# Two early weights converted and split beside the bit steps of attention, with smaller head pools

## The chip, the cores and the metric

The kernel runs on one core of a Trainium2 chip. The metric is device microseconds (us) from the first to the last work of one launch, the median of several runs. Five engines take part, each with its own queue that runs in order: PE (TensorE, matmuls; PEld is its weight load), DVE (VectorE), ACT (ScalarE), POOL (GpSimd) and SP (SyncE, which only issues DMAs here).

## The reference

A hash-masked attention over 2 x 8 heads, 768 positions and 64 channels feeds a gated layer (d_ff 1536) and then a layer with h * cos(h) (d_ff 2048). Weights of the two layers come as float64.

```python
q_bits = (np.einsum('bhsd,dk->bhsk', q, proj) > 0)      # 6 bits a position: its bucket
mask = q_bucket[:, :, :, None] == k_bucket[:, :, None, :]
scores = np.where(mask, scale * np.matmul(q, k.transpose(0, 1, 3, 2)), -1000000000.0)
attn = softmax(scores)                                  # max taken off, sum + 1e-9
x = np.matmul(attn, v)                                  # 2 x 8 x 768 x 64 -> 1536 x 512
gate = 1.0 / (1.0 + np.exp(-(x @ w_gate)))
x = (gate * (x @ w_val)) @ w_out                        # first layer
h = x @ w_in
out = (h * np.cos(h)) @ w_out2                          # second layer
```

## The kernel before

The kernel has two parts, `attention()` and `moe()`, and in both each engine's order of work is the order of the code (a manual schedule); only at the border of the two are matmuls of `moe()` set between the last ones of `attention()`.

**Attention** walks through 96 steps `g`, six for each of 16 heads; one step handles 128 query rows against 768 keys. In a step PE makes the scores of step g + 2 (`scores`, L456 and L459), DVE takes the row minimum of step g + 1 (`rowmax`, tile `mn`, L467), ACT the exponential (`expo`, tile `p`, L474), and POOL normalises three steps later (`norm`, L507, in place on `p`). Seven steps later (`LAG`) PE transposes the normalised tiles (`ptrans`, tile `t`, L523), ACT rounds the transpose to its high part `ph` (L528), DVE subtracts it to get the low part `pl` (L533), and PE multiplies both with the values (`pv`, tile `o`, L543 and L544). Three `p` tiles make one unit of six transposes, and the first transpose of a unit needs all three normalised. When a unit is done ACT copies `o` out (`fin_act`, tile `e`, L553); there is one `o` buffer, so the next unit's first matmul waits for that copy. When two heads are done, POOL adds the halves (`fin_sum`, tile `ef`, L580), ACT rounds them into the high half of `xy` (`fin_hi`, L596) and POOL subtracts for the low half (`fin_lo`, L600).

**Preparing a head** hd (loads `nqk`, transposes `pt`, the bits) is spread over earlier steps by the tables `LOAD_AT`, `TRANS_AT`, `BITS_AT`. At step 6 hd - 8 PE makes the six matmuls of the bits (tile `pb`, L341); one step later DVE turns them into codes (tile `bf`, L326) and SP sends them into the head's tiles with four small DMAs (L363). Six more DMAs (`place`, L323) move the transposed q and k into these tiles. DMAs share eight completion counters in turn, and each waits for the DMA that had its counter before.

**The order within a step** is the list `ORDER` (L21): `Tb LOa ... EXP Ta MIN LATE W HIb ...`. `MIN` is the row minimum, `HIb` a rounding to `ph`, `LATE` the codes, and `W` is `early_weights` (L731).

**Early weights.** A weight tile is loaded as float64 words (`load_raw`), converted (`convert_parts`: ACT makes `wp`, L151; DVE makes `wl`, L155, and joins them into `w`, L160) and split (`wsplit`: ACT rounds to the high part `gh` or `vh`, L123; a subtraction makes `gl` or `vl`, L124). The first two weights are `g0` and `v0`. Before, they are loaded at steps 72 and 74, converted at steps 84 to 92 and split by `moe()`, whose pool `wsp` opens only there:

```python
            WL, WC = (72, 74, 76), 84
            WSTEP = 4
```

**moe()** is a list of items, twelve or more matmuls each (L805, L867, L922), with all conversions and splits in between.

Of the kernel before, what the change touches and what calls it, by code (L numbers as in the profile page):

```python
# [9 lines left out]
F32 = mybir.dt.float32  # L10
F32R = mybir.dt.float32r
# [3 lines left out]
ALU = mybir.AluOpType  # L15
# [3 lines left out]
P = 128  # L19

ORDER = (  # L21
    "Tb LOa COEF NRM PVb EXP Ta MIN LATE W HIb PVa PREP S FIN HIa PVaF LOb".split()
)
LAST = ["COEF", "NRM"] + [name for name in ORDER if name not in ("COEF", "NRM")]
FILL = "COEF NRM MIN EXP LATE W PREP S".split()
# [15 lines left out]
def lsh_attention_glu_moe_cos_moe(  # L41
# [80 lines left out]
    def split(dst_h, dst_l, src, sub):  # L122
        nc.scalar.copy(dst_h, src)  # L123
        sub.tensor_tensor(out=dst_l, in0=src, in1=dst_h.bitcast(F32), op=ALU.subtract)  # L124
# [20 lines left out]
    def convert_parts(key):  # L145
        nm, f, _ = key
        rw = raws.pop(key)
        words = rw.bitcast(I32).rearrange("p (n two) -> p n two", two=2)
        lw, hw = words[:, :, 0], words[:, :, 1]
        pt = wraw.tile([P, 512], F32, tag="wp", name=f"wp_{nm}{f}", bufs=2)  # L150
        nc.scalar.activation(  # L151
            pt, hw.bitcast(F32), AF.Prelu, scale=float(2.0**-112), alpha=float(2.0**32)
        )
        lt = wraw.tile([P, 512], I32, tag="wl", name=f"wl_{nm}{f}", bufs=2)
        nc.vector.tensor_scalar(  # L155
            out=lt, in0=lw, scalar1=29, scalar2=7, op0=ALU.logical_shift_right, op1=ALU.bitwise_and
        )
        yield
        w = wraw.tile([P, 512], F32, tag="we", name=f"w_{nm}{f}", bufs=NWE)
        nc.vector.scalar_tensor_tensor(  # L160
            out=w.bitcast(I32),
            in0=pt.bitcast(I32),
            scalar=3,
            in1=lt,
            op0=ALU.logical_shift_left,
            op1=ALU.bitwise_or,
        )
        wt[key] = w
# [51 lines left out]
    def load_to(n, eng=nc.sync):  # L220
        nonlocal loaded
        while loaded < min(n, len(order)):
            load_raw(order[loaded], eng)
            loaded += 1


    def attention():
        nonlocal done
        parts = None
        with ExitStack() as st:  # L230
            nat = st.enter_context(tc.tile_pool(name="nat", bufs=3))
            prep = st.enter_context(tc.tile_pool(name="prep", bufs=3))
            vsp = st.enter_context(tc.tile_pool(name="vsp", bufs=3))
            pp = st.enter_context(tc.tile_pool(name="pp", bufs=10))
            tiny = st.enter_context(tc.tile_pool(name="tiny", bufs=3))
# [357 lines left out]

            def fin_hi(u):
                for h, _, x in pieces(u):
                    nc.scalar.copy(h, x)  # L596

            def fin_lo(u):
                for h, lw, x in pieces(u):
# [1 line left out]

            LAG = 7

            WL, WC = (72, 74, 76), 84
            WSTEP = 4
            NW = 2 * NG

            todo = {}
# [21 lines left out]
                at(s1 + VALUES_AT[hd % 2], lambda hd=hd: values(hd))  # L630

            late = []

            def run_late():
                now = late[:]
# [33 lines left out]
            with tc.manual_schedule(  # L669
# [50 lines left out]
                for g in range(NG + LAG + 2):  # L720
# [8 lines left out]
                            at(g + LOW_AT + (3 if g < NG <= g + LOW_AT else 0), lambda u=fin: fin_lo(u))  # L729

                    def early_weights():  # L731
                        nonlocal done, parts
                        if g in WL:
                            load_to(1 + WL.index(g), nc.scalar)
                        if done < NEARLY and g >= WC and (g - WC) % WSTEP == 0:
                            parts = convert_parts(order[done])
                        if parts is not None and next(parts, parts) is parts:
                            parts = None
                            done += 1
                        elif parts is None and 0 < done <= NEARLY:  # L740
                            load_to(done + 3, nc.scalar)

                    def norms():
                        for n in range(g - 3, NG if g == NG else g - 2):
# [23 lines left out]
                        "PREP": (True, lambda: run_todo(g)),  # L768
                        "HIa": (0 <= wa + 2 < NW, lambda: phi(wa + 2)),
                    }  # L770
                    for name in ORDER if LAG - 1 <= g != NG else LAST if g == NG else FILL:
                        on, fn = ops[name]
                        if on:
                            fn()
# [3 lines left out]

    def moe():
        with ExitStack() as st:  # L780
            wsp = st.enter_context(tc.tile_pool(name="wsp", bufs=2))
            wk = st.enter_context(tc.tile_pool(name="wk", bufs=2))
            gsp = st.enter_context(tc.tile_pool(name="gsp", bufs=(NC - 1) * F2))
            wk2 = st.enter_context(tc.tile_pool(name="wk2", bufs=2))
            ps_h = st.enter_context(tc.tile_pool(name="ps_h", bufs=4, space=PSUM))
            ps_a = st.enter_context(tc.tile_pool(name="ps_a", bufs=1, space=PSUM))

            ws = {}

            def wsplit(key):  # L790
                nm, f, again = key
                role = ROLE[nm]
                nb = 3 if role == "c" else 2
                h = wsp.tile([P, KT, P], F32R, tag=role + "h", name=f"{nm}h{again}_{f}", bufs=nb)
                lw = wsp.tile([P, KT, P], F32R, tag=role + "l", name=f"{nm}l{again}_{f}", bufs=nb)
                sub = nc.vector if key in (("g", 0, 0), ("g", 1, 0), ("v", 1, 0)) else nc.gpsimd
                split(h, lw, wt.pop(key).rearrange("p (k c) -> p k c", k=KT), sub)
                ws[key] = (h, lw)

            def proj_in(ps, c, key):  # L800
                wh, wl = ws[key]
# [144 lines left out]
                split_at[kk] = max(soon, convert_at.get(k, -1) + 1)  # L946
                assert split_at[kk] <= use[kk]
            for kk in sorted(order, key=lambda kk: use[kk] - lead(kk)[1]):
                due[split_at[kk]].append(lambda kk=kk: wsplit(kk))
            for k, n in convert_at.items():  # L950
                due[n].append(lambda k=k: convert_to(k + 1))

# [63 lines left out]
```

## Time and profile before

| | before |
|---|---|
| runs | 801.29 us, median of 3 (801.16 to 801.84) |
| profiled execution | 801.07 us, span 799.3 us |
| PE busy | 789.1 us, 99% of the span |
| ACT, DVE, POOL busy | 468.9, 508.5, 321.4 us |
| window 20 to 200 us (attention) | PE 179.78, DVE 156.49, ACT 165.51, POOL 155.38 of 180 us busy |
| granted TensorE clock | 1.00 throughout |

The span runs from the first to the last instruction; 1.8 us of the profiled time lie outside it. Attention ends near 243 us, and the two layers take the rest. PE matmuls overlap in the records (each is shown longer than the distance to the next), so that a busy PE says little; the distance between two starts, and what ended a wait of PEld, say more.

### The profile page before, as it was taken

The page shows a single profiled execution, that of the slowest core. Times are in us where ns is not written, and L with a number is a line of the kernel's source. Part 1 is how long each engine was busy: PE and PEld are TensorE (multiplying, and loading weights), DVE is VectorE, ACT ScalarE, POOL GpSimd, SP SyncE. Part 2 cuts the span into 40 slices and gives each one's busy share as a digit, 9 for nine tenths or more (in the row PEclk, how much of TensorE's full clock was granted, in tenths as well). Part 3 has the DMA queues.
Part 4 walks back from the last instruction along what each step waited for, and adds up shares of the span by engine and source line. Part 5 has one row for each costly group of instructions (what it writes and reads, how often), then busy time and mean ns, then how long its engine had stood idle before and what let it go on. Part 6 is the DMA issues. An engine that isn't in the chain of part 4 may idle for free.

```text
span 799.3 us, 11621 instructions
## 1 busy us (share of the span) xinstructions
PE 789.1 (99%) x3984; PEld 677.5 (85%) x3984; DVE 508.5 (64%) x797; ACT 468.9 (59%) x932; POOL 321.4 (40%) x343
## 2 busy tenths in 40 slices
PE   7999999999999999999999999999999999999998
PEld 5999999999998888888888888888888888888886
DVE  7888888888985443334443266657655666676662
ACT  7999989989985332222332244456666656664442
POOL 5779988988871222222222112221222122222221
PEclk9999999999999999999999999999999999999999
DMA  6865675587413433222221122323223333242312
GB/s 168 207 159 140 159 186 142 143 207 194 112 52 100 129 115 100 80 79 80 80 80 53 53 72 86 115 71 120 89 82 105 106 106 103 82 157 81 105 53 105
DMA packets 70890, 89.03 MB, mean 111 GB/s; under 512 B 30128, under 2 KB 55088, under 8 KB 70832
## 3 DMA queue, kind: packets, MB, share of 16 engines
q1 hardware_dynamic: 67504, 85.30, 37.5%
q10 hardware_dynamic: 3328, 3.00, 1.4%
q8 instruction: 31, 0.51, 0.3%
q14 instruction: 27, 0.22, 0.1%
HBM read 59.77 MB, written 3.15 MB: 79 GB/s over the span
## 4 chain that ended last, share of the span: by engine, by line
PE 97%; DVE 1%; ACT 1%; DMA 0%; issue 0%; SPq 0%; ACTq 0%; DVEq 0%
PE ph L805 16%; PE a L922 16%; PE pg L805 12%; PE pv L805 12%; PE a L867 12%; PE t L523 8%; PE o L543 4%; PE o L544 4%; PE s L456 4%; PE s L459 4%; PE pb L341 2%; PE pt L284 1%; PE a L898 1%; ACT p L474 1%; DMA pj<-in_proj 0%; DVE mn L467 0%
## 5 line engine op out<-in xcount | busy, mean ns | idle before, releaser
L805 PE MATMUL ph<-xy,ih 128*128 128x512 f32 x384 | 118.2, 389 | 0.0
L123 ACT CAST gh<-g 128x512 fp32r<-128x512 f32 x84 | 52.1, 620 | 110.1 <-PE a L922 43.8
L533 DVE TENSOR_TENSOR pl<-t,ph 128x384 fp32r<-128x384 f32 x192 | 102.7, 552 | 16.9 <-ACT ph L528 15.1
L124 POOL TENSOR_TENSOR zl<-w_z,zh 128x512 fp32r<-128x512 f32 x32 | 41.4, 1295 | 166.7 <-ACT zh L123 166.7
L507 POOL TENSOR_SCALAR p<-p,r,d 128x768 f32<-128x768 f32 x96 | 94.8, 992 | 22.1 <-PE s L459 7.6
L831 DVE TENSOR_TENSOR g<-pv,sg 128x512 f32<-128x512 f32 x36 | 24.9, 691 | 120.0 <-PE pv L805 120.0
L528 ACT CAST ph<-t 128x384 fp32r<-128x384 f32 x192 | 90.7, 485 | 17.5 <-PE t L523 16.0
L467 DVE TENSOR_REDUCE mn<-s 128x1 f32<-128x770 f32 x96 | 91.1, 950 | 12.4 <-PE s L459 9.7
L523 PE MATMUL t<-ident,p 128*128 128x128 f32 x576 | 94.9, 272 | 0.0
L124 DVE TENSOR_TENSOR gl<-g,gh 128x512 fp32r<-128x512 f32 x84 | 57.8, 688 | 53.0 <-ACT gh L123 50.8
L474 ACT ACTIVATE p<-s,mn 128x768 f32<-128x768 f32 x96 | 88.2, 918 | 2.7 <-DVE mn L467 2.5
L805 PE MATMUL pg<-xy,gh 128*128 128x512 f32 x288 | 89.3, 390 | 0.0
L805 PE MATMUL pv<-xy,vh 128*128 128x512 f32 x288 | 88.7, 389 | 0.0
L829 ACT ACTIVATE sg<-pg 128x512 f32<-128x512 f32 x36 | 21.4, 593 | 111.8 <-PE pg L805 111.8
L805 PEld LDWEIGHTS ph<-xy,ih 128*128 128x128 f32 x384 | 72.1, 188 | 15.0
L523 PEld LDWEIGHTS t<-ident,p 128*128 128x128 f32 x576 | 74.8, 140 | 8.0 <-POOL p L507 0.3
L543 PE MATMUL o<-ph,vs 128*128 128x384 f32 x192 | 79.1, 412 | 0.3 <-ACT e L553 0.3
L805 PE MATMUL ph<-xy,il 128*128 128x512 f32 x192 | 74.7, 389 | 0.0
L922 PE MATMUL a<-zh,gl 128*128 128x512 f32 x184 | 71.7, 390 | 0.0
L922 PE MATMUL a<-zh,gh 128*128 128x512 f32 x184 | 71.6, 389 | 0.0
L922 PE MATMUL a<-zl,gh 128*128 128x512 f32 x184 | 71.6, 389 | 0.0
L456 PE MATMUL s<-k,q 96*128 96x384 f32 x192 | 69.2, 360 | 2.3 <-ACT p L474 2.0
(119 smaller groups left out, 1747.4 us busy)
## 6 DMA issues: line engine op xcount, KB each, us to landing
raw_z<-in_moe_w_out SPq DMA_DIRECT2D x32, 512.0 KB, 3.3
raw_o<-in_moe_w_out SPq DMA_DIRECT2D x23, 512.0 KB, 3.3
q<-x SPq DMA_DIRECT2D x45, 192.0 KB, 3.8
k<-x SPq DMA_DIRECT2D x45, 192.0 KB, 3.7
raw_i<-in_moe_w_in SPq DMA_DIRECT2D x16, 512.0 KB, 4.0
raw_g<-in_moe_w_gate SPq DMA_DIRECT2D x10, 512.0 KB, 3.6
raw_v<-in_moe_w_val SPq DMA_DIRECT2D x10, 512.0 KB, 3.5
nv<-in_v SPq DMA_DIRECT2D x8, 384.0 KB, 3.8
```

Source lines behind the costliest of these rows:

```text
L124: sub.tensor_tensor(out=dst_l, in0=src, in1=dst_h.bitcast(F32), op=ALU.subtract)
L456: nc.tensor.matmul(o, hh["q2"][0:96, t, :], hh["k2"][0:96, sl, :], start=True, stop=False)
L467: nc.vector.tensor_reduce(mn_t[u][:, i : i + 1], s_t[g][:, :, 0 : HS + 1], axis=AX.XY, op=ALU.min)
L474: nc.scalar.activation(pt, s_t.pop(g)[:, :, 0:HS], AF.Exp, bias=mn_t[u][:, i : i + 1], scale=-1.0, accum_out=sm_t[u][:, i : i + 1],)
L507: nc.gpsimd.tensor_scalar(out=pt, in0=pt, scalar1=r[:, i : i + 1], scalar2=d[:, i : i + 1], op0=ALU.mult, op1=ALU.add,)
L523: nc.tensor.transpose(pt[:, i, :], pv_[:, j * P : (j + 1) * P], ident)
L528: nc.scalar.copy(ph, pt_t[w])
L533: nc.vector.tensor_tensor(out=pl, in0=pt_t.pop(w), in1=ph_t[w].bitcast(F32), op=ALU.subtract)
L543: nc.tensor.matmul(o_t[u], vs[:, j, :], ph_t.pop(w), start=(j == 0), stop=False)
L805: nc.tensor.matmul(ps, w[:, kt, :], xy[c][:, hl, kt, :], start=(n == 0), stop=(n == 11))
L867: nc.tensor.matmul(acc[c, e], w[:, e, :], m, start=(f == 0 and n == 0), stop=(f == F1 - 1 and n == 2),)
L922: nc.tensor.matmul(acc[c, t], m[:, ts], w, start=(f == 0 and n == 0), stop=(f == F2 - 1 and n == 2),)
```

## The change

- `g0` and `v0` are loaded at steps 29 and 47 (three more weights at 65, 71 and 83, on ACT's queue as before), converted at steps 41, 47 and 59, 65, 71, and split at 53, 59 and 77, 83. All these steps are 6 hd - 7, the one after a head's bit matmuls. In these steps the order is `ROOM`, where `W` stands ahead of `MIN` and `LATE`.
- `wp` and `wl` are now two parts, with a `yield` in between.
- The split tiles of the roles a and b (gate and value weights) have pools that live from the start; `v0`'s subtraction moves from POOL to DVE.
- The pools `nat` and `prep` have two buffers instead of three.
- For the pair that ends with unit 27 (head 13) the rounding into `xy` is done by POOL instead of ACT.

```diff
@@ -20,6 +20,9 @@
 
 ORDER = (
     "Tb LOa COEF NRM PVb EXP Ta MIN LATE W HIb PVa PREP S FIN HIa PVaF LOb".split()
+)
+ROOM = (
+    "Tb LOa COEF NRM PVb EXP Ta W MIN LATE HIb PVa PREP S FIN HIa PVaF LOb".split()
 )
 LAST = ["COEF", "NRM"] + [name for name in ORDER if name not in ("COEF", "NRM")]
 FILL = "COEF NRM MIN EXP LATE W PREP S".split()
@@ -151,6 +154,7 @@
         nc.scalar.activation(
             pt, hw.bitcast(F32), AF.Prelu, scale=float(2.0**-112), alpha=float(2.0**32)
         )
+        yield
         lt = wraw.tile([P, 512], I32, tag="wl", name=f"wl_{nm}{f}", bufs=2)
         nc.vector.tensor_scalar(
             out=lt, in0=lw, scalar1=29, scalar2=7, op0=ALU.logical_shift_right, op1=ALU.bitwise_and
@@ -224,12 +228,31 @@
             loaded += 1
 
 
+    ws = {}
+    pools = {r: ctx.enter_context(tc.tile_pool(name="ws" + r, bufs=2)) for r in "ab"}
+
+    def wsplit_parts(key):
+        nm, f, again = key
+        role = ROLE[nm]
+        h, lw = (
+            pools[role].tile([P, KT, P], F32R, tag=role + x, name=f"{nm}{x}{again}_{f}") for x in "hl"
+        )
+        src = wt.pop(key).rearrange("p (k c) -> p k c", k=KT)
+        nc.scalar.copy(h, src)
+        yield
+        sub = nc.vector if key in (("g", 0, 0), ("v", 0, 0), ("g", 1, 0), ("v", 1, 0)) else nc.gpsimd
+        sub.tensor_tensor(out=lw, in0=src, in1=h.bitcast(F32), op=ALU.subtract)
+        ws[key] = (h, lw)
+
+    def wsplit(key):
+        for _ in wsplit_parts(key):
+            pass
+
     def attention():
         nonlocal done
-        parts = None
         with ExitStack() as st:
-            nat = st.enter_context(tc.tile_pool(name="nat", bufs=3))
-            prep = st.enter_context(tc.tile_pool(name="prep", bufs=3))
+            nat = st.enter_context(tc.tile_pool(name="nat", bufs=2))
+            prep = st.enter_context(tc.tile_pool(name="prep", bufs=2))
             vsp = st.enter_context(tc.tile_pool(name="vsp", bufs=3))
             pp = st.enter_context(tc.tile_pool(name="pp", bufs=10))
             tiny = st.enter_context(tc.tile_pool(name="tiny", bufs=3))
@@ -593,7 +616,12 @@
 
             def fin_hi(u):
                 for h, _, x in pieces(u):
-                    nc.scalar.copy(h, x)
+                    if u == 2 * NH - 5:
+                        nc.gpsimd.tensor_scalar(
+                            out=h, in0=x, scalar1=1.0, scalar2=1.0, op0=ALU.mult, op1=ALU.mult
+                        )
+                    else:
+                        nc.scalar.copy(h, x)
 
             def fin_lo(u):
                 for h, lw, x in pieces(u):
@@ -601,8 +629,8 @@
 
             LAG = 7
 
-            WL, WC = (72, 74, 76), 84
-            WSTEP = 4
+            W_LOAD = {29: 1, 47: 2, 65: 3, 71: 4, 83: 5}
+            W_STEPS = {41: "01", 47: "1", 53: "2", 59: "30", 65: "1", 71: "1", 77: "2", 83: "3"}
             NW = 2 * NG
 
             todo = {}
@@ -630,6 +658,7 @@
                 at(s1 + VALUES_AT[hd % 2], lambda hd=hd: values(hd))
 
             late = []
+            early = {}
 
             def run_late():
                 now = late[:]
@@ -729,16 +758,16 @@
                             at(g + LOW_AT + (3 if g < NG <= g + LOW_AT else 0), lambda u=fin: fin_lo(u))
 
                     def early_weights():
-                        nonlocal done, parts
-                        if g in WL:
-                            load_to(1 + WL.index(g), nc.scalar)
-                        if done < NEARLY and g >= WC and (g - WC) % WSTEP == 0:
-                            parts = convert_parts(order[done])
-                        if parts is not None and next(parts, parts) is parts:
-                            parts = None
-                            done += 1
-                        elif parts is None and 0 < done <= NEARLY:
-                            load_to(done + 3, nc.scalar)
+                        nonlocal done
+                        for part in W_STEPS.get(g, ""):
+                            key = order[done]
+                            if part == "0":
+                                early["c"] = convert_parts(key)
+                            if part == "2":
+                                early["s"] = wsplit_parts(key)
+                            next(early["s" if part > "1" else "c"], None)
+                            done += part == "3"
+                        load_to(W_LOAD.get(g, 0), nc.scalar)
 
                     def norms():
                         for n in range(g - 3, NG if g == NG else g - 2):
@@ -768,7 +797,8 @@
                         "PREP": (True, lambda: run_todo(g)),
                         "HIa": (0 <= wa + 2 < NW, lambda: phi(wa + 2)),
                     }
-                    for name in ORDER if LAG - 1 <= g != NG else LAST if g == NG else FILL:
+                    steps = ORDER if LAG - 1 <= g != NG else LAST if g == NG else FILL
+                    for name in ROOM if g in W_STEPS else steps:
                         on, fn = ops[name]
                         if on:
                             fn()
@@ -778,24 +808,12 @@
 
     def moe():
         with ExitStack() as st:
-            wsp = st.enter_context(tc.tile_pool(name="wsp", bufs=2))
+            pools["c"] = st.enter_context(tc.tile_pool(name="wsc", bufs=3))
             wk = st.enter_context(tc.tile_pool(name="wk", bufs=2))
             gsp = st.enter_context(tc.tile_pool(name="gsp", bufs=(NC - 1) * F2))
             wk2 = st.enter_context(tc.tile_pool(name="wk2", bufs=2))
             ps_h = st.enter_context(tc.tile_pool(name="ps_h", bufs=4, space=PSUM))
             ps_a = st.enter_context(tc.tile_pool(name="ps_a", bufs=1, space=PSUM))
-
-            ws = {}
-
-            def wsplit(key):
-                nm, f, again = key
-                role = ROLE[nm]
-                nb = 3 if role == "c" else 2
-                h = wsp.tile([P, KT, P], F32R, tag=role + "h", name=f"{nm}h{again}_{f}", bufs=nb)
-                lw = wsp.tile([P, KT, P], F32R, tag=role + "l", name=f"{nm}l{again}_{f}", bufs=nb)
-                sub = nc.vector if key in (("g", 0, 0), ("g", 1, 0), ("v", 1, 0)) else nc.gpsimd
-                split(h, lw, wt.pop(key).rearrange("p (k c) -> p k c", k=KT), sub)
-                ws[key] = (h, lw)
 
             def proj_in(ps, c, key):
                 wh, wl = ws[key]
@@ -946,7 +964,8 @@
                 split_at[kk] = max(soon, convert_at.get(k, -1) + 1)
                 assert split_at[kk] <= use[kk]
             for kk in sorted(order, key=lambda kk: use[kk] - lead(kk)[1]):
-                due[split_at[kk]].append(lambda kk=kk: wsplit(kk))
+                if kk not in ws:
+                    due[split_at[kk]].append(lambda kk=kk: wsplit(kk))
             for k, n in convert_at.items():
                 due[n].append(lambda k=k: convert_to(k + 1))
 
```

The first place is DVE in step 47 of attention, between two `pl` subtractions and the row minimum. Before:

```order
L533 TENSOR_TENSOR pl_1949<-t_1912,ph_1928 128x384
L533 TENSOR_TENSOR pl_1955<-t_1923,ph_1944 128x384
L467 TENSOR_REDUCE mn_1967<-s_99 128x1
L326 TENSOR_SCALAR bf_1970<-pb_1930,bcode 128x384
L533 TENSOR_TENSOR pl_1988<-t_1951,ph_1976 128x384
```

After, at the same place (serial numbers and line numbers differ, the tiles are the same):

```order
L556 TENSOR_TENSOR pl_1961<-t_1924,ph_1940 128x384
L556 TENSOR_TENSOR pl_1967<-t_1935,ph_1956 128x384
L164 SCALAR_TENSOR_TENSOR w_g_1979<-wp_g_1733,wl_g_1735 128x512
L490 TENSOR_REDUCE mn_1983<-s_105 128x1
L349 TENSOR_SCALAR bf_1986<-pb_1942,bcode 128x384
L556 TENSOR_TENSOR pl_2004<-t_1963,ph_1992 128x384
```

One DVE instruction on a weight now stands between the `pl` pair and `mn`. Steps 41, 59, 65, 71 and 83 gain one at the same place (`wl_g`, `gl`, `wl_v`, `w_v`, `vl`), so two fall to even heads (41 and 65) and four to odd heads.

The second place is ACT in step 84, where the rounding of a pair into `xy` falls. Before:

```order
L474 ACTIVATE p_3441,sm_3408<-s_99,mn_3407 128x768
L151 ACTIVATE wp_g_3448<-raw_g_2968 128x512
L528 CAST ph_3452<-t_3428 128x384
L596 CAST xy_70<-ef_3024 128x256
L596 CAST xy_71<-ef_3024 128x512
L528 CAST ph_3464<-t_3443 128x384
```

After:

```order
L497 ACTIVATE p_3471,sm_3438<-s_105,mn_3437 128x768
L551 CAST ph_3478<-t_3458 128x384
L624 CAST xy_70<-ef_3052 128x256
L624 CAST xy_71<-ef_3052 128x512
L551 CAST ph_3490<-t_3473 128x384
```

The conversion `wp_g` has left this place; `wp_v`, which stood between two `p` of step 88, has left too.

The third place is POOL at the end of attention, behind the last normalisation. Before:

```order
L507 TENSOR_SCALAR p_3804<-p_3804,r_3819,d_3820 128x768
L600 TENSOR_TENSOR xy_70<-ef_3493,xy_70 128x256
L600 TENSOR_TENSOR xy_71<-ef_3493,xy_71 128x512
L124 TENSOR_TENSOR vl_0_4021<-w_v_3621,vh_0_4020 128x512
L580 TENSOR_TENSOR ef_3863<-e_3786,ef_3863 128x384
```

After:

```order
L530 TENSOR_SCALAR p_3818<-p_3818,r_3833,d_3834 128x768
L620 TENSOR_SCALAR xy_70<-ef_3517 128x256
L620 TENSOR_SCALAR xy_71<-ef_3517 128x512
L628 TENSOR_TENSOR xy_70<-ef_3517,xy_70 128x256
L628 TENSOR_TENSOR xy_71<-ef_3517,xy_71 128x512
L603 TENSOR_TENSOR ef_3877<-e_3800,ef_3877 128x384
```

Two roundings came and the subtraction `vl` went. SP's order is the same in both kernels.

## Rows read from the trace of the kernel before

**Rows 1.** The profile's chain that ended last, shares of the span by engine.

```profile
PE 97%; DVE 1%; ACT 1%; DMA 0%; issue 0%; SPq 0%; ACTq 0%; DVEq 0%
```

**Rows 2.** Waits of PEld, 20 to 205 us: total us, times, longest.

```profile
PEld o L543 <- ACT e L553: 1.5, 5, 0.3
```

**Rows 3.** Waits of PEld, 205 to 217 us, all of them.

```profile
PEld s L456 <- ACT p L474: 0.5, 1, 0.5
PEld o L543 <- ACT e L553: 0.3, 1, 0.3
PEld o L544 <- DVE pl L533: 0.2, 1, 0.2
```

**Rows 4.** Timeline of PE, steps 84 and 85: start us, us, operation.

```profile
207.91 0.49 PE L523 MATMUL t<-ident,p 128*128 128x128 f32 x3
208.63 0.44 PE L456 MATMUL s<-k,q 96*128 96x384 f32 x1 [0.23 <-ACT p L474]
...
209.84 0.49 PE L523 MATMUL t<-ident,p 128*128 128x128 f32 x3
210.09 0.42 PE L543 MATMUL o<-ph,vs 128*128 128x384 f32 x1
```

**Rows 5.** Timeline of ACT, step 84.

```profile
205.43 0.68 ACT L151 ACTIVATE wp_g<-raw_g 128x512 f32<-128x512 f32 x1
206.00 0.48 ACT L528 CAST ph<-t 128x384 fp32r<-128x384 f32 x1
```

**Rows 6.** Waits of PEld, 217 to 246 us, for the copy of `o`.

```profile
PEld o L543 <- ACT e L553: 1.1, 3, 0.6
```

**Rows 7.** Timeline of ACT in step 47; in brackets its idle time and who ended it.

```profile
116.81 0.30 ACT L484 ACTIVATE sm<-sm,small 128x3 f32<-128x3 f32 x1
117.69 0.48 ACT L528 CAST ph<-t 128x384 fp32r<-128x384 f32 x1 [0.58 <-PE t L523]
```

**Rows 8.** Timeline of DVE in step 47.

```profile
115.92 0.56 DVE L533 TENSOR_TENSOR pl<-t,ph 128x384 fp32r<-128x384 f32 x1 [0.21 <-ACT ph L528]
117.08 0.96 DVE L467 TENSOR_REDUCE mn<-s 128x1 f32<-128x770 f32 x1 [0.60 <-PE s L459]
```

**Rows 9.** Timeline of POOL in steps 47 and 48.

```profile
116.37 0.99 POOL L507 TENSOR_SCALAR p<-p,r,d 128x768 f32<-128x768 f32 x1
117.32 1.85 POOL L580 TENSOR_TENSOR ef<-e,ef 128x768 f32<-128x768 f32 x1
119.14 1.00 POOL L507 TENSOR_SCALAR p<-p,r,d 128x768 f32<-128x768 f32 x1
```

**Rows 10.** The chain that ended last, 118 to 132 us: start, us, what.

```profile
119.40 0.33 PE t L523 x3
...
120.08 0.45 PE t L523 x3
```

**Rows 11.** Timeline of all engines, 206.9 to 210.9 us.

```profile
209.06 0.91 DVE L160 SCALAR_TENSOR_TENSOR w_g<-wp_g,wl_g 128x512 int32<-128x512 int32 x1
...
209.41 2.39 POOL L507 TENSOR_SCALAR p<-p,r,d 128x768 f32<-128x768 f32 x2
```

**Rows 12.** Timeline of DVE, a conversion while POOL is idle.

```profile
217.88 0.67 DVE L160 SCALAR_TENSOR_TENSOR w_v<-wp_v,wl_v 128x512 int32<-128x512 int32 x1
```

**Rows 13.** The page's costliest groups: busy, mean ns of one, idle before.

```profile
L507 POOL TENSOR_SCALAR p<-p,r,d 128x768 f32<-128x768 f32 x96 | 94.8, 992 | 22.1 <-PE s L459 7.6
```

**Rows 14.** Waits of SP's queue, 176 to 184 us.

```profile
SPq L256 <- DMA raw_g<-in_moe_w_gate: 2.7, 1, 2.7
```

**Rows 15.** Timeline of SP: codes of head 9 sent at step 47.

```profile
119.26 1.22 SPq L363 DMA_DIRECT2D k<-bf  x2
```

**Rows 16.** Timeline of PE: first scores of head 9.

```profile
130.58 0.34 PE L456 MATMUL s<-k,q 96*128 96x384 f32 x1
```

**Rows 17.** DMA issues, 60 to 200 us: KB each, median us to landing.

```profile
raw_v<-in_moe_w_val ACTq DMA_DIRECT2D x1, 512.0 KB, 6.3
```

**Rows 18.** Timeline of PE at the start, first wait behind head 2's transposes.

```profile
12.01 0.44 PE L456 MATMUL s<-k,q 96*128 96x384 f32 x1 [1.06 <-ACT p L474]
```

**Rows 19.** Timeline of POOL at the end of attention.

```profile
241.47 1.02 POOL L580 TENSOR_TENSOR ef<-e,ef 128x384 f32<-128x384 f32 x1 [3.72 <-DMA e<-e]
```

## The prediction

> **What bounds the kernel now.** The chain of work that ended last is read first: it is PE for 97% [rows 1], so a change counts only where it adds or removes a wait of PE. PEld's waits tell where these are. In steady attention (20 to 205 us) nearly all are one kind, five waits of 0.3 us for the copy of `o` [rows 2], one behind each rounding of a pair into `xy`. Where the weight conversions stand, 205 to 217 us, three waits make 1.0 us [rows 3]. Behind that, up to the layers, three waits for the copy of `o` remain [rows 6]; no early weight stands on ACT just ahead of the longest, so I leave these as they are. The two layers are PE without gaps and the change does not touch their order. So at most some 1.0 us can be won; what can be lost depends on what the moved instructions meet in steps 41 to 83, and there the timelines of ACT, DVE and POOL around step 47 are read.
>
> **What is removed at steps 84 to 88.** `wp_g` sits on ACT ahead of a `ph` and two roundings into `xy`. From its start to that of the next ACT instruction pass 0.57 us (205.43 to 206.00) [rows 5]. PE pays soon after: between three transposes and the next matmul lie 0.25 us normally (209.84 to 210.09), but 0.72 at 207.91 [rows 4], so 0.47 us are lost to the late `p`. Without `wp_g` all that ACT does there comes 0.57 earlier, and this wait goes. The wait for `pl` (0.2) lies just behind `w_g`, which held DVE for 0.91 us [rows 3, 11]; the wait for the copy of `o` at step 88 (0.3) lies behind `wp_v` [rows 3]. A weight-load wait overstates what PE loses a little, since loads run ahead of their matmuls. The three give 0.7 to 1.0 us; I take **-0.9**.
>
> **What is added on ACT, steps 41, 53, 59 and 77.** Each gets one conversion or rounding of 512 columns, 0.57 us from start to start as above. In step 47, which stands for all steps behind the bits, ACT idles 0.58 us before `ph`, because PE is busy with the bits [rows 7]; the new instruction stands exactly there. Cost 0. If that gap were gone, ACT would be 0.57 late, and PE would lose up to 0.47 as at step 84. The five loads are issued in the same gap.
>
> **What is added on DVE, steps 41, 47, 59, 65, 71 and 83.** Here DVE idles 0.60 us between `pl` and `mn` [rows 8], and a joining takes 0.67 when nothing else disturbs it [rows 12]. Taken alone this costs nothing either: `mn` would move by a tenth, and ACT is not ready for it yet. But POOL is in the way. At 209.06 the same DVE instruction took 0.91 rather than 0.67, and the two normalisations that POOL began at 209.41 took 2.39 rather than 2 x 0.992 = 1.98 [rows 11, 12, 13]: DVE waited for POOL's earlier instruction to end, and POOL then lost 0.41 to DVE. The Trainium skill, "SBUF — State Buffer", section "Who interferes with whom", says that a DVE instruction with two SBUF inputs or in a two-port mode shares a port pair with GpSimd as an exclusive lock, so that the other fully blocks for the whole instruction. By this rule each such meeting would cost POOL the whole DVE instruction, and the sum below would be +1.4 rather than +0.3; the trace's 0.41 agrees in kind, not in size.
>
> Who waits for POOL? In an odd head's step POOL runs without a gap: a normalisation from 116.37, the addition `ef` from 117.32 and the last normalisation of a unit from 119.14 to 120.14 [rows 9]. In the chain the three transposes at 120.08 take 0.45 instead of the 0.33 of those at 119.40 [rows 10]: the third needs that last `p`. So POOL has no slack there and already costs PE 0.12. The new DVE instruction wants to start about 116.40, where the second `pl` (115.92 + 0.48) lets go [rows 8], so it falls among these three POOL instructions whichever goes first. POOL ends the unit 0.41 later, and PE's third transpose waits that long. Steps 47, 59, 71 and 83 are of this kind: 4 x 0.41 = **+1.6**. From below it is 0, if POOL makes it up; from above 4 x 0.67 = 2.7, if the whole instruction blocks. I take 0.41, since it is measured on the same pair of instructions. Steps 41 and 65 are even heads, without the addition, so POOL reaches the unit's last normalisation with time to spare; I take 0, at most 0.41 each.
>
> While PE waits 0.41 there, ACT catches up, so the 0.3 us wait of the weight load behind the following `xy` rounding [rows 2] falls away. PE's own share of it is about half, 0.13; three times (the one after step 83 is already in the 0.9): **-0.4**.
>
> **The buffers.** With two `nqk` buffers the load of head 2 waits until head 0 is transposed. It is behind the transposes that the first wait at 12.01 comes, and in it PE idles 1.06 us for `p` anyway [rows 18]; the load may be some tenths later. Cost 0, at most 0.3. With two buffers of `prep` the moves of q and k wait for the last scores of the head two before; those stand in the same step, and the data is wanted about six steps later. Cost 0.
>
> **The end of attention.** POOL takes two roundings and gives up `vl`. It idles 3.72 us before the last addition [rows 19], more than two roundings of 768 columns together (one normalisation of 768 columns takes 0.992 [rows 13]). ACT gives up three groups there, but PE has matmuls of the layer to put in, and does not wait for ACT there in the rows except for the copies of `o`. Between -0.2 and +0.2; I take 0.
>
> **The sum.** -0.9 + 1.6 - 0.4 = +0.3 us on the profiled 801.07, so 801.4 for such an execution. The median of the runs is 0.2 above the profiled one; **801.6 us** is forecast for the median. A difference under 0.2%, 1.6 us, can hardly be told from none.
>
> **Rivals.**
> - *POOL's delay doesn't arrive.* If POOL and DVE interleave without loss, or POOL's wait comes from something else that moves too, the sum is -0.9 - 0.1 and the median about 800.4. For it: the only conversion rows stand in one stretch, where POOL was not critical. Against it: the third transpose starts as the normalisation ends in every odd head's step.
> - *The whole DVE instruction blocks POOL.* Then 4 x 0.67 - 0.9 - 0.4 = +1.4, and a late `mn` (DVE itself waits up to 0.93 for the normalisation from 116.37 to 117.32 to end) may add a tenth or two each: 802.7 to 803.3. This is what the Trainium skill's rule from above would give.
> - *Slower by the sends.* The weight load is given the completion counter that the third or fourth small send of the same step must wait for. Before, SP waited 2.7 us for a weight in such a way [rows 14], and a weight took 6.3 us to land [rows 17]. Now `k<-bf`, issued at 119.26 [rows 15], would wait to about 117.0 (behind `sm` [rows 7]) + 6.3 = 123.3, and the head's scores come at 130.58 [rows 16]: some 7 us for two issues and a landing, enough. It decides only if a weight takes above 10 us to land; then each microsecond more, in up to five steps, is one for PE: 803.5 or more.
> - *More is won.* If the longest wait for the copy of `o` (0.6) went as well and ACT's lighter load at the end of attention saved the rest of these 1.1 us [rows 6], with no loss on POOL: -0.9 - 0.9 = -1.8, about 799.5. Against it: the copy waits for PE's own last product and not for a weight.
>
> **How the numbers follow.** Chances: forecast 0.45 (its own range 801.0 to 802.2), no delay on POOL 0.27, full block 0.17, sends 0.06, more won 0.05. The range 800.2 to 803.0 leaves out the last two and the upper part of the full block. Faster by over 0.2% (under 799.7) is the last case and a little of the second: 0.06. Slower by over 0.2% (above 802.9) is the sends and less than half of the full block: 0.13. The remainder is 0.81.
>
> **What would show it.** Right: PEld has no waits for `p` or `pl` near 206 to 211 us; in steps 47, 59, 71 and 83 the transposes behind `ef` show a wait of PE for POOL's normalisation of 0.4 us, and POOL's `ef` there lasts some 0.4 longer or starts that much later; ACT's gap of 0.58 is filled in steps 41, 53, 59 and 77. Wrong: no wait for POOL there (then faster), or waits of scores for the codes' DMAs, or new waits at steps 41 and 65.

## The result, and the profile after

The changed kernel takes 807.38 us, the median of 8 runs (803.58 to 810.48), against 801.18 (801.08 to 801.84, 8 runs) for the kernel before on the same chip: ratio 1.0075, 95% interval 1.0062 to 1.0088. It is slower by 6 us where 801.6 was forecast, and outside the range of 800.2 to 803.0.

Its profiled execution took 810.48 us (span 808.7), 9.4 more than before. It is the longest of the eight; a second profile, below, is of one that took 805.84. First the chain that ended last, shares of the span by engine. It answers to [rows 1]: PE no longer makes nearly all of it.

```profile
PE 89%; DMA 3%; POOL 3%; ACT 2%; DVE 1%; issue 1%; SPq 1%; POOLq 0%; ACTq 0%; DVEq 0%
```

The waits of PEld, 20 to 215 us (line and tile, what ended the wait: total us, times, longest), answer to [rows 2, 3].

```profile
PEld t L546 <- POOL p L530: 7.4, 5, 3.1
PEld s L479 <- ACT p L497: 0.7, 2, 0.5
PEld o L566 <- ACT e L576: 0.3, 1, 0.3
```

The first line is new: the transposes wait for POOL's normalisation. The second is not: the kernel before has the same two waits, near 20 us. The wait for the copy of `o` fell from 1.5 to 0.3. The waits for `p`, `pl` and the copy at 205 to 217 us [rows 3] are gone too (that stretch is now some 9 us later, and up to 226 us none of them appears), so what the change was costed to remove is removed. The timeline of PE has two of the new waits that are far longer than the others, in brackets; the last line is one of three short ones, and lies behind the window above:

```profile
94.81 0.47 PE L546 MATMUL t<-ident,p 128*128 128x128 f32 x1 [2.92 <-DMA q<-x]
...
186.21 0.47 PE L546 MATMUL t<-ident,p 128*128 128x128 f32 x1 [2.47 <-POOL p L530]
...
216.50 0.33 PE L546 MATMUL t<-ident,p 128*128 128x128 f32 x1 [0.42 <-POOL p L530]
```

Each is the third transpose of a unit; two go ahead of it, so not a unit's first transpose but its third needs the last normalised tile. The first long one is put down to a transfer `q<-x`, since that ended last by the profile; but this matmul reads `p`, and POOL's `p` ended at 94.76 (below), 0.05 us before it. A name in brackets is the last event, not always the one needed. The table by stretch has, behind PE's share, the granted clock (the number ahead of the DMA share):

```profile
core 0: us, PE busy (x) PEld busy (x) DVE busy (x) ACT busy (x) POOL busy (x), PEclk, DMA share, GB/s
91.50:94.80 3.30, 0.37 (x2) 0.14 (x1) 0.81 (x2) 1.02 (x3) 2.78 (x3) 0.84 1.01 230
94.80:100.60 5.80, 5.79 (x22) 5.50 (x23) 2.35 (x4) 3.61 (x8) 5.58 (x7) 0.50 0.37 83
183.40:186.20 2.80, 0.34 (x3) 0.10 (x1) 1.05 (x2) 1.21 (x3) 2.76 (x2) 0.95 1.06 275
186.20:189.60 3.40, 3.39 (x14) 3.20 (x15) 0.87 (x2) 1.86 (x4) 3.26 (x5) 0.54 0.35 77
189.60:200.00 10.40, 10.40 (x72) 10.04 (x71) 8.96 (x15) 9.70 (x23) 9.48 (x12) 1.00 0.55 135
```

PE stands still for about 3 us, and then, fully busy, runs at the lower of its two levels (1.2 GHz, a clock of 0.50) for 5.8 us, and for 3.4 us at 0.54 in the second place. That loses 5.8 x 0.50 + 3.4 x 0.46 = 4.5 us more. By PE's own idle time the five waits for POOL make 2.92 + 0.42 + 0.39 + 2.47 + 0.42 = 6.6 us. With the 4.5 of the clock, and less the 0.9 and 0.4 that the forecast has as removed, that is 9.8 us, close to the 9.4 found.

**Why POOL is late.** POOL's timeline ahead of the first wait:

```profile
85.16 1.01 POOL L328 TENSOR_TENSOR x<-xf,x 128x384 fp32r<-128x384 f32 x1
88.93 0.51 POOL L288 TENSOR_SCALAR vs<-nv 128x384 fp32r<-128x384 f32 x1 [2.76 <-DMA nv<-in_v]
...
91.99 1.80 POOL L603 TENSOR_TENSOR ef<-e,ef 128x768 f32<-128x768 f32 x1 [0.48 <-DMA e<-e]
93.78 0.98 POOL L530 TENSOR_SCALAR p<-p,r,d 128x768 f32<-128x768 f32 x1
```

It waits for two transfers: the load `nv` of the next values, and the move of `e` to the partitions of its pair. With `nv` late, the addition `ef` has only 0.48 us left to wait for `e`: the two are late nearly alike. Ahead of the second long wait, `e` alone is late:

```profile
183.38 1.80 POOL L603 TENSOR_TENSOR ef<-e,ef 128x768 f32<-128x768 f32 x1 [1.86 <-DMA e<-e]
```

In the kernel before, the first place's two instructions stand here, with no wait ahead of them:

```profile
86.17 0.51 POOL L265 TENSOR_SCALAR vs<-nv 128x384 fp32r<-128x384 f32 x1
...
88.72 1.85 POOL L580 TENSOR_TENSOR ef<-e,ef 128x768 f32<-128x768 f32 x1
```

**Why the transfers are late.** The chain of the changed kernel, 70 to 100 us, in order of time (start, us, what):

```profile
74.05 7.31 DMA raw_g<-in_moe_w_gate
81.36 0.02 issue
81.38 0.51 SPq L386
...
81.93 1.28 SPq L386
...
83.25 0.61 SPq L279
...
83.96 0.58 SPq L272
```

The weight load of step 29 lands after 7.31 us, and only then does SP issue the third send of head 6's codes (L386), which must wait for the load's completion counter. Behind it stand the fourth send, the load `nqk` (L279) and `nv` (L272). The waits of SP's queue, 20 to 215 us, say the same, one held send for a gate weight in each of steps 29 and 65, one for a value weight (step 47) and one for an out weight (step 71); behind 215 us the load of step 83 holds a move of `e` for 3.1 us:

```profile
SPq L386 <- DMA raw_g<-in_moe_w_gate: 5.8, 2, 3.7
...
SPq L386 <- DMA raw_v<-in_moe_w_val: 3.6, 1, 3.6
...
SPq L386 <- DMA raw_o<-in_moe_w_out: 3.4, 1, 3.4
```

SP issues the move of `e` at 85.92, and right behind it the first of six moves of q and k for the next head (timeline of SP):

```profile
85.92 0.59 SPq L590 DMA_DIRECT2D e<-e  x1
86.62 0.57 SPq L346 DMA_DIRECT2D q<-x  x1
```

In the kernel before `nv` and `e` were issued some 4.1 us earlier:

```profile
79.85 0.58 SPq L249 DMA_DIRECT2D nv<-in_v  x1
...
81.82 0.59 SPq L567 DMA_DIRECT2D e<-e  x1
```

Landing (the DMA issues, last figure: median us from issue), before:

```profile
nv<-in_v SPq DMA_DIRECT2D x1, 384.0 KB, 3.5
...
e<-e SPq DMA_DIRECT2D x1, 192.0 KB, 4.3
```

and in the changed kernel:

```profile
nv<-in_v SPq DMA_DIRECT2D x1, 384.0 KB, 4.8
...
e<-e SPq DMA_DIRECT2D x1, 192.0 KB, 5.9
```

The weight itself is not what slows these two: it had landed at 74.05 + 7.31 = 81.36, before either was issued. They now move together with the next head's moves, with a DMA share of 1.06 from 86 to 92 us; before, `e` had nearly landed when the first of those was issued (85.14), with a share of 0.82. That the slower landing comes from this company is inferred, not tested.

So `e` was there at 81.82 + 4.3 = 86.1 and wanted at 88.72: 2.6 us to spare. Now it is issued 4.1 later and takes 1.6 longer, 5.7 against 2.6: 3.1 us too late, which is PE's wait. For `nv` the slack was 86.17 - (79.85 + 3.5) = 2.8, and the lateness 4.1 + 1.3 = 5.4, so 2.6 too late: POOL waits 2.76.

### The profile page after: what moved, and what is told of

Its sections match the earlier page's. It is cut to its first block, busy times and chain, and to the rows that moved or that the text cites. A ratio compares the mean times of both kernels' runs of the same rounds, so it can differ in the third digit from the quotient of the medians.

```text
span 808.7 us, 11621 instructions
## 1 busy us (share of the span) xinstructions
PE 792.2 (98%) x3984; PEld 682.0 (84%) x3984; DVE 510.7 (63%) x798; ACT 470.6 (58%) x930; POOL 322.2 (40%) x344
## 4 chain that ended last, share of the span: by engine, by line
PE 89%; DMA 3%; POOL 3%; ACT 2%; DVE 1%; issue 1%; SPq 1%; POOLq 0%; ACTq 0%; DVEq 0%
PE ph L823 16%; PE a L940 15%; PE pg L823 12%; PE pv L823 12%; PE a L885 12%; PE t L546 6%; PE o L566 3%; PE s L479 3%; PE o L567 3%; PE s L482 3%; POOL p L530 2%; PE pb L364 1%; PE pt L307 1%; ACT p L497 1%; DMA raw_g<-in_moe_w_gate 1%
## 5 line engine op out<-in xcount | busy, mean ns | idle before, releaser
L546 PE MATMUL t<-ident,p 128*128 128x128 f32 x576 | 96.8, 275 | 6.7 <-POOL p L530 3.7
```

The costliest lines, as they stand in the source:

```text
L546: nc.tensor.transpose(pt[:, i, :], pv_[:, j * P : (j + 1) * P], ident)
```

## The experiments

Three theories. **Theory 1**: a weight's counter holds SP, and what is queued behind the held send is late for POOL. **Theory 2**: GpSimd and VectorE disturb each other in the odd heads' steps. **Theory 3**: with two buffers the places of q and k wait for scores and hold SP. All runs are compared with the kernel before on the same chip, and each "before" was 800.93 to 801.08 us.

**The loads moved.**

```diff
-            W_LOAD = {29: 1, 47: 2, 65: 3, 71: 4, 83: 5}
+            W_LOAD = {37: 1, 49: 2, 61: 3, 73: 4, 85: 5}
```

> The changed kernel with nothing altered but the steps in which the five weights are loaded: 37, 49, 61, 73 and 85 (was 29, 47, 65, 71 and 83). There the next user of a load's completion counter is a place or an ef move some steps later, not a send of the same step. Theory 1 (SP's queue is held by a weight's counter, and the head's low-part load and e move behind it come late for POOL): the waits of PE's transposes for POOL's normalisation near 91 and 183 us go, the granted clock is 1.00, and the time is that of my sum, 801 to 802. Theory 2 (GpSimd and VectorE disturb each other in the odd heads' steps): no change against the changed kernel, 805 to 808. Theory 3 (with two buffers the places of q and k wait for scores and hold SP): no change either, 805 to 808.

Measured 801.35 (801.18 to 801.50, 11 runs), ratio 1.0003 (0.9994 to 1.0012), clock 1.00. The two long waits are gone; PEld's waits for POOL are the four short ones (20 to 215 us):

```profile
PEld t L546 <- POOL p L530: 2.5, 4, 0.6
```

Five numbers give back 6.0 of the 6.2 us; theories 2 and 3 can't have them.

**The loads alone**, in the kernel before:

```diff
-            WL, WC = (72, 74, 76), 84
+            WL, WC = (29, 47, 65), 84
```

> The kernel before with one change: its three weight loads stand in steps 29, 47 and 65, where a send of the same step is next on the load's counter (was 72, 74 and 76); three buffers, the conversions at steps 84 to 88. Theory 1: slower by 2 to 6 us with waits of PE for POOL's normalisation some 17 us behind one or more of the three loads, 803 to 807. Theory 2: no change, 800.8 to 801.6, since no weight instruction runs in steps 41 to 83. Theory 3: no change, since the buffers are three.

Measured 806.73 (803.30 to 809.77, 6 runs), ratio 1.0074 (1.0053 to 1.0095). With three buffers, conversions where they were and nothing else changed, the whole loss is there. PEld's waits, 20 to 215 us:

```profile
PEld t L523 <- POOL p L507: 6.5, 4, 2.9
```

**The buffers alone**, in the kernel before:

```diff
-            nat = st.enter_context(tc.tile_pool(name="nat", bufs=3))
-            prep = st.enter_context(tc.tile_pool(name="prep", bufs=3))
+            nat = st.enter_context(tc.tile_pool(name="nat", bufs=2))
+            prep = st.enter_context(tc.tile_pool(name="prep", bufs=2))
```

> The kernel before with two buffers in nat and prep instead of three, nothing else. Theory 1: within 0.3 us of before. Theory 2: the same. Theory 3: slower by 3 us or more, as the places of q and k now wait for the scores of the head two before and hold what is queued behind them on SP.

Measured 801.09, ratio 1.0001 (0.9992 to 1.0009). Theory 3 falls, and the prediction's 0 for the buffers holds.

**The rounding alone**: the kernel before with the branch for `u == 2 * NH - 5` of the diff above in `fin_hi`.

> The kernel before with the one pair's rounding on POOL and nothing else changed. My sum has it at nothing, between -0.2 and +0.2: 800.8 to 801.4. If the rounding delays POOL's last additions or frees ScalarE at the end of attention, it is outside of this.

Measured 801.20, ratio 1.0002 (0.9993 to 1.0010): nothing, as costed.

**The weight instructions in even heads' steps**, loads away from the sends:

```diff
-            W_LOAD = {29: 1, 47: 2, 65: 3, 71: 4, 83: 5}
-            W_STEPS = {41: "01", 47: "1", 53: "2", 59: "30", 65: "1", 71: "1", 77: "2", 83: "3"}
+            W_LOAD = {13: 1, 37: 2, 61: 3, 73: 4, 85: 5}
+            W_STEPS = {17: "01", 29: "1", 35: "2", 41: "3", 47: "0", 53: "1", 65: "1", 71: "2", 77: "3"}
```

> The changed kernel with loads at 13, 37, 61, 73 and 85 and the weight instructions of VectorE and POOL's rounding moved to even heads' steps (17, 29, 41, 53, 65, 77; ScalarE's alone remain at 35, 47 and 71). Theory 1 with the port conflict of my sum: a's gain, and in addition the 1.2 to 1.6 us of the odd heads' steps: 800 to 800.6, faster than a by about a microsecond. Theory 1 without a port conflict: the same as a within 0.3. Theory 2: this one alone of the four comes down from 805 or more to 800 or 801. Theory 3: no change against the changed kernel.

Measured 800.01 (799.83 to 800.89, 11 runs), ratio 0.9988 (0.9979 to 0.9996): below both kernels, if by less than the 1.6 us that the prediction said can hardly be told from none. (The edit moves the instructions of VectorE and ScalarE; POOL's rounding, which the expectation names too, stays where it was.) Against the kernel with only the loads moved it is 1.34 us less. That is what POOL and DVE cost PE in the odd heads' steps, below called the port term. In the kernel with only the loads moved, in step 47, POOL's timeline reads (answering to [rows 9]):

```profile
116.30 1.49 POOL L530 TENSOR_SCALAR p<-p,r,d 128x768 f32<-128x768 f32 x1
117.75 1.84 POOL L603 TENSOR_TENSOR ef<-e,ef 128x768 f32<-128x768 f32 x1
119.57 0.99 POOL L530 TENSOR_SCALAR p<-p,r,d 128x768 f32<-128x768 f32 x1
```

DVE's joining stands beside the first of them:

```profile
116.31 0.70 DVE L164 SCALAR_TENSOR_TENSOR w_g<-wp_g,wl_g 128x512 int32<-128x512 int32 x1
```

And in the kernel with the even heads POOL has the first one undisturbed:

```profile
116.30 0.98 POOL L530 TENSOR_SCALAR p<-p,r,d 128x768 f32<-128x768 f32 x1
```

The 0.70 us of DVE lengthen POOL's 0.98 by 0.51; in the three other odd heads' steps it takes 1.49 to 1.50 too. `ef` starts 0.5 later, and PE idles 0.40, 0.41, 0.39 and 0.40 for `p` in these four steps, 1.6 us (2.5 by PEld), and not at all with the even heads. There three waits for the copy of `o` are back instead, so that the net is less than 1.6.

**Which loads?** PE waits long behind steps 29 and 65 only, though SP is held behind 47, 71 and 83 too. Steps 29 and 65 are those of heads 6 and 12, the others of odd heads. `nv` and the two moves for a pair's addition stand behind an even head's sends; behind an odd head's stand only `nqk` and a move of `e` that is wanted much later. Three kernels try this. Two loads three steps later:

```diff
-            W_LOAD = {29: 1, 47: 2, 65: 3, 71: 4, 83: 5}
+            W_LOAD = {32: 1, 47: 2, 68: 3, 71: 4, 83: 5}
```

> The changed kernel with two of its five loads moved by three steps: those of steps 29 and 65, which share their step with the sends of an even head, to 32 and 68, behind the sends. The loads of 47, 71 and 83, which share theirs with an odd head's sends, stay. Theory 1 as the rows now read (a held send costs only where the load of the low parts and the two moves for a pair's addition stand behind it on SP, that is behind an even head's sends): the two long waits of PE go and the time is that of the kernel with all loads moved, 801.0 to 801.7, though SP still waits for a weight in three steps. Rival (any held send costs, or the five transfers as such do): 803 to 807.

Measured 802.19 (801.67 to 805.53, 11 runs), ratio 1.0018 (1.0009 to 1.0026): most of the loss is gone, but 0.8 us more than with all loads moved. `e` is issued on time here (81.77), yet it lands slowly (4.2 us with all loads moved). The weight, issued at 81.7 and landed at 89.2, moves with it:

```profile
e<-e SPq DMA_DIRECT2D x1, 192.0 KB, 7.9
```

POOL's addition then waits,

```profile
89.78 1.84 POOL L603 TENSOR_TENSOR ef<-e,ef 128x768 f32<-128x768 f32 x1 [0.73 <-DMA e<-e]
```

and PE 0.93 us behind it. So a weight also costs by moving at the same time, which my expectation left out. At the second place ScalarE waits 1.04 us for the gate weight's counter before it can issue the out weight's load, and PE idles 0.59 rather than 0.39.

All loads with the sends of odd heads:

```diff
-            W_LOAD = {29: 1, 47: 2, 65: 3, 71: 4, 83: 5}
+            W_LOAD = {23: 1, 47: 2, 59: 3, 71: 4, 83: 5}
```

> The changed kernel with all five loads in steps that share them with an odd head's sends: 23, 47, 59, 71 and 83. Theory 1 as the rows now read: SP waits 3 us or more for a weight in five steps, PE waits for none of it, 801.0 to 802.0. Rival (each held send costs PE something, whatever stands behind it): as slow as the changed kernel or slower, 805 to 812.

Measured 801.46 (801.31 to 801.76, 11 runs), ratio 1.0005 (0.9996 to 1.0014). SP is held five times, as its queue's waits show (four sends, and at L587 a move of `e`),

```profile
SPq L386 <- DMA raw_g<-in_moe_w_gate: 8.4, 2, 5.1
...
SPq L386 <- DMA raw_v<-in_moe_w_val: 3.6, 1, 3.6
SPq L587 <- DMA raw_v<-in_moe_w_val: 3.1, 1, 3.1
SPq L386 <- DMA raw_o<-in_moe_w_out: 3.0, 1, 3.0
```

and PE pays nothing for it beyond the port term.

All loads with the sends of even heads:

```diff
-            W_LOAD = {29: 1, 47: 2, 65: 3, 71: 4, 83: 5}
+            W_LOAD = {29: 1, 41: 2, 53: 3, 65: 4, 77: 5}
```

> The changed kernel with all five loads in steps that share them with an even head's sends: 29, 41, 53, 65 and 77. Theory 1: the two places of the changed kernel cost 6.0 us together (807.4 against 801.35); five of them, or four if one falls behind the sends, cost 12 to 15: 813 to 817, with four or five waits of PE of about 3 us each for POOL's normalisation and a lower clock behind some. Rival (the two loads cost for another reason that has to do with steps 29 and 65 alone): about 807.

Measured 807.27 (803.94 to 808.34, 6 runs), ratio 1.0067 (1.0054 to 1.0080). The place is right, the price is not. Its waits of PEld, 20 to 215 us:

```profile
PEld t L546 <- POOL p L530: 8.1, 5, 2.1
```

Four of the five places wait long, with 1.85, 1.62, 1.48 and 1.55 us of idle time of PE; at the fifth it is `nv` itself that is held, for 2.4 us, and PE idles 0.39, no more than the port term makes. Only behind the first did the clock drop (0.68 from 93.7 to 99.0; 1.00 behind the three others). I had multiplied a price that held two stretches at the lower clock and longer waits: here SP issued the first place's `e` at 85.38 and it landed in 5.4 us, against 85.92 and 5.9 in the profile of the changed kernel. The idle time, 6.5 us, less 0.4 of the port term in three of the steps, and 5.3 x 0.32 us of clock make 7.0, which is what the profiled execution (808.34) has over the kernel with the loads moved (801.35).

**What is wanted behind the held send?** In the changed kernel, at the first place alone, the two moves of `e` (head 3), the load `nv` (head 6), or both go to ScalarE's queue:

```diff
-                    nc.sync.dma_start(f_t[hd // 2][64:128], e[64:128])
-                    nc.sync.dma_start(e_t[hd - 1][64:128], e[0:64])
+                    eng = nc.scalar if hd == 3 else nc.sync
+                    eng.dma_start(f_t[hd // 2][64:128], e[64:128])
+                    eng.dma_start(e_t[hd - 1][64:128], e[0:64])
```

> The changed kernel with the two moves of head 3's e (the first of the two places where PE waits long) issued on ScalarE's queue instead of SP's; the value load nv stays on SP behind the held send, and the second place is left as it is. If POOL needs both, this alone gives little: POOL's values are still held by nv, and PE's wait near 91 us stays at 2 to 3 us. If the e moves alone are what comes late, that wait falls to about 1 us or less. Time: 805 to 808 in the first case, 2 to 5 us less than the changed kernel in the second.

Measured 806.83 (803.53 to 811.63, 6 runs), ratio 1.0086 (1.0054 to 1.0118); the profiled execution is the shortest, 803.53. In it POOL goes from `nv` (still issued at 83.97) to `ef` without a wait, PE idles 0.23 at 93.05. But ScalarE stood still for a counter:

```profile
81.70 0.48 ACT L551 CAST ph<-t 128x384 fp32r<-128x384 f32 x1 [1.35 <-DMA q<-bf]
```

That made POOL itself late: its normalisation ahead of the values starts at 85.11 instead of 83.61 in the changed kernel. So this run does not show that an `nv` of that lateness is harmless.

> The changed kernel with the one value load nv behind the first held send issued on ScalarE's queue; the two e moves stay on SP. If POOL needs both, POOL's wait of 2.8 us for nv goes, its addition then waits for e about as long, and PE's wait near 91 us stays at 2 to 3 us; 805 to 808. If nv alone is what comes late, the wait falls to about 1 us or less.

```diff
-                    at(max(s1 + LOAD_AT["v"], -1), lambda hd=hd: load(hd, "v"))
+                    at(
+                        max(s1 + LOAD_AT["v"], -1),
+                        lambda hd=hd: load(hd, "v", eng=nc.scalar if hd == 6 else nc.sync),
+                    )
```

(with `eng.dma_start` in `load`). Measured 803.42 (802.79 to 804.70, 6 runs), ratio 1.0032 (1.0020 to 1.0043). POOL's values are on time, and its addition waits for `e` instead:

```profile
90.69 1.81 POOL L603 TENSOR_TENSOR ef<-e,ef 128x768 f32<-128x768 f32 x1 [2.10 <-DMA e<-e]
```

PE idles 2.02 for it: the row is as expected if POOL needs both, but the time is below the 805 to 808 that I gave; in the profiled execution the clock stayed at 1.00 and PE idled only 0.66 at the second place. A late `e` alone makes two thirds of the wait, though it is issued 0.7 us and lands 1.3 us earlier here than in the changed kernel.

> Both edits: nv and the two e moves of the first place on ScalarE's queue, so nothing that POOL needs there stands behind the held send, while SP is held as long as in the changed kernel and the weight moves at the same time. Theory 1: PE's wait near 91 us falls to 1.2 us or less and that stretch keeps its clock; 2 to 5 us less than the changed kernel, 802.5 to 805.5. If the weight's transfer itself (its share of the DMA engines) is what delays PE, the wait stays at 2 to 3 us. The ScalarE queue may have to wait for a counter too; then ScalarE's own work is late and PE waits for it instead.

Both edits: 808.21 (807.73 to 810.44, 4 runs), ratio 1.0093 (1.0078 to 1.0109). This does not free the place: the move of `e` now needs a counter that `nv` holds, and ScalarE stands still.

```profile
ACT ph L551 <- DMA nv<-in_v: 4.6, 1, 4.6
```

PE waits 3.5 us for `ph` in place of POOL. So of these three runs only the one with `nv` moved speaks clearly: with the values on time, the late `e` still holds POOL and PE. What `nv` alone would cost is not shown, since in the other two moving `e` to another queue moved the stall too.

**The changed kernel again**, for a second profile:

> The changed kernel itself once more, for a second profile: its first profiled execution was the longest of eight. Theory 1: the same two waits of PE for POOL's normalisation, near 91 and 183 us, of 1.5 to 3.2 us each, and the difference to the first profile lies in how long PE then runs at the lower clock.

805.84 us. The long wait at the first place is there (2.67 us idle), that of the second only 0.70. Between 94.3 and 98.0 the mean clock is 0.70: it is 1.00 up to 95.5, and 0.50 from 96 to 99. So the cost of the second place differs between executions of one kernel (2.47 and 0.70), and so does the clock behind the first; that the second place lies near the edge of its slack is inferred. The time varies with the clock: of the eight timed runs the two at a mean clock of 1.00 took 803.58 and 804.41, the six at 0.993 to 0.997 took 806.43 to 810.48.

## Why the prediction was wrong

All its terms but one held. Without the loads' places the sum of +0.3 was measured as 801.35 - 801.06 = +0.3, with an interval of -0.5 to +1.0. Point by point:

- **Removed at steps 84 to 88, -0.9**: the even heads' kernel, which has this gain and hardly a port meeting, is 801.06 - 800.01 = 1.05 us faster than before (0.3 to 1.7). Right.
- **Added on ACT, 0**: no new wait of PE for ACT appeared in the profile after. Right.
- **POOL and DVE, +1.6, and -0.4 of absorbed waits**: net 1.2; measured 1.34, and PE's idle time in the four steps is the 1.6. One meeting lengthens POOL's instruction by 0.51 rather than the 0.41 taken. Three of the five waits for the copy of `o` went as forecast (1.5 to 0.6 with the loads moved; in the changed kernel a fourth is hidden behind the long wait at 94.8). The Trainium skill, "SBUF — State Buffer", section "Who interferes with whom", has the lock held for the whole DVE instruction, 0.70 here; 0.51 lies between its price and mine.
- **The buffers and the rounding, 0 each**: 801.09 and 801.20 against 801.06 and 801.08. Right.
- **The sends: the step that failed.** The rival *Slower by the sends* had the mechanism, the third or fourth send waiting for the weight's counter, and got 0.06. It named the head's scores as what waits behind, 7 us away, and made 10 us of landing the point from which it decides. Landing was 7.3 us, and it decided. The fault is in the place that was read: step 47 "stands for all steps behind the bits", but two of the five loads stand with an even head, where `nv` and the moves of `e` are queued behind the same send. At step 29 these had 2.8 and 2.6 us to spare, less than the 4.1 us by which SP issued them late. For the odd heads, step 47 among them, the argument was right, as the kernel shows in which SP is held five times at no cost. I listed who waits for the sends, and not who else stands behind them on SP.
- **Its size**: the weight was given 6.3 us from a load elsewhere; in the changed kernel, beside the moves of q and k and the sends, it took 6.9 to 7.9. And a wait of 3 us was priced as 3 us, without the stretch at the lower clock behind it.

At the first place 4.1 of `e`'s 5.7 us of lateness are issue and 1.6 are landing, behind a weight that had landed already; how the 6.0 us divide over both places and all executions stays open.

One sum is off without a consequence: the rival without a delay on POOL, -0.9 - 0.1, gives 800.3 rather than 800.4.

## What to carry to other kernels

When a DMA is added to another queue, ask which later DMA is next on its completion counter, and then go through everything queued behind that one, at every place where it happens: each has a slack of its own (wanted time less issue less landing), and the smallest decides. Moving the loads to steps where no short deadline stands behind them gave all of it back; a load three steps later, which moved together with a wanted transfer, gave back most. And a place read as an example must be checked for what alternates: here even and odd heads.

## What the runs showed of the hardware

- A 512 KB weight load landed in 3.4 to 5.1 us in the two kernels with all loads away from the sends, and in 6.9 to 7.9 in the changed kernel. A 192 KB move of `e` took 7.9 us beside a weight load, instead of 4.3; issued late, behind the weight and among the next head's moves, it took 5.9.
- DVE's 0.70 us on two SBUF operands, started 0.01 to 0.03 us behind a normalisation of POOL, lengthened that one from 0.98 to 1.49 or 1.50, four times out of four.
- After waits of PE of 2.9 and 2.5 us the granted clock was 0.50 and 0.54 for 5.8 and 3.4 us; in another execution, after 2.7 us, it was 0.50 from 96 to 99. In the kernel with the even heads' loads it fell behind a wait of 1.85 and was 1.00 behind waits of 1.5 to 1.6; in the one with `nv` moved it was 1.00 behind a wait of 2.0. The time of the changed kernel spreads over 7 us, where the kernel before spreads over 0.8; the two of its eight runs at a clock of 1.00 are the fastest.
